# Decay attention and mixture of experts on one core: the listed order of all steps and the buffers laid out anew

## The chip, the core and the metric

The kernel runs on one core of a Trainium2 chip. The metric is the device time of one execution in microseconds; shorter is better. The core has five engines with queues of their own: TensorE (PE in the rows; PEld is its loading of weights, which overlaps the matmuls), VectorE (DVE), ScalarE (ACT), GpSimd (POOL) and SyncE (SP), which here only issues transfers. An engine takes its queue in order; an instruction that waits for another engine holds up all that stand behind it on its own.

## The reference

Attention with a decay over 8 batches of 8 heads (576 positions, 64 wide), and on its output a mixture of 4 experts, of which each position takes 2, each an attention of its own. Cut to what matters:

```python
# attention: q, k, v (8, 8, 576, 64), f (8, 8, 576)
scores = scale * np.matmul(q, k.transpose(0, 1, 3, 2))
cum = np.cumsum(np.log(np.clip(f, 0.0001, 1.0)), axis=-1)
scores = np.where(causal, -1000000000.0, scores + cum[..., :, None] - cum[..., None, :])
attn = softmax(scores)
x = np.matmul(attn, v)                      # laid out as (8, 576, 512)
# experts: top 2 of 4 by x @ w_gate, w = softmax over the two logits
for e in range(4):
    q, k, v = x @ wq[e], x @ wk[e], x @ wv[e]
    a = softmax(np.where(causal, -1000000000.0, scale * (q @ k.T)))
    ye = a @ v @ wo[e]
    for kk in range(2):
        out += (topk[:, :, kk] == e)[..., None] * w[:, :, kk:kk + 1] * ye
```

## The kernel before

The work is cut into 48 units. 32 are a batch and a pair of heads (a0_0 to a7_3: batch, pair), 16 a batch and a pair of experts (m0_0 to m7_1). The experts of a batch come one batch behind its heads. Each unit goes through the same steps, and each step is a Python generator, a task:

- `prep_attn` (L396) loads xin (L401), copies halves of it with ScalarE (L404, L407; L410 only in the first two units) and takes the rounding remainders with two VectorE operations of 64 partitions each (L416). Their two halves, near and far, start on partition 0 and on partition 64, in one order or the other. SP copies halves within SBUF (L394) and adds rows for the decay (L386 for the first unit, L390 for the others). `prep_moe` (L526) does the like for experts, with matmuls pp_m (L542).
- `max_pass` (L563) finds each row's maximum: matmuls m0, m1, m2, m3 (all L571, shown as m_a or m_m), each followed by a VectorE reduction (L577, with a short read of its accumulator under the same line, and L592, L624, L631), then a transpose mp on TensorE (L636) and a copy ms on ScalarE (L639).
- `scores` (L660) multiplies again (L670, L671), exponentiates on ScalarE (L687 to L726), masks on GpSimd (L657, L690, L728) and adds up the blocks there (L734 to L740).
- `attend` (L746) multiplies by the values: oa and ob (both L759). `row_sums` (L789) and `apply_rows` (L840) divide a group of two units by its sums: matmuls sm (L798), VectorE L812 to L830, ScalarE L832, L869, VectorE L850, L877.
- `moe_front` (L429) makes the experts' values (pv, L445) and gates (L464 to L523). `project_out` (L881) multiplies by wo (po, L893), copies to outb with ScalarE (L900) and stores (L903, L906).

Beside the units, `load_weights` loads and splits the weights (st_v, st_k and so on: SP L359, ScalarE L363, GpSimd L365), and `keep_warm` (L215) issues 150 matmuls on zeros (warm, L218) that nobody reads.

What sets the order is no scheduler but a table. ORDER is a string of two-digit numbers to the base 64; each names a task and advances it by one step, to its next `yield` (4w is `keep_warm`, 00 the `prep_attn` of a0_0, 4A `load_weights`). A loop behind it makes every instruction depend on the one before it on its engine, so that each engine's queue stands as listed. SLOTS says, for each kind of tile, which of its buffers the next allocation takes; an allocation waits until the last reader of that buffer is done. Both tables come from a replay of the program outside of the kernel; the kernel holds only its result.

```python
digits = "".join(ORDER.split())
for x, y in zip(digits[::2], digits[1::2]):
    i = DIGITS.index(x) * len(DIGITS) + DIGITS.index(y)
    if i not in started:
        started[i] = iter(tasks[i]())
    next(started[i], None)
```

Of the kernel before, what the change touches and what calls it, by code (L numbers as in the profile page):

```python
# [1003 lines left out]
```

## Time and profile before

| | us |
|---|---|
| runs of the kernel before | 703.61, 706.12, 706.38 |
| their median | 706.12 |
| the profiled execution | 704.02 |
| its span, first to last instruction | 702.3 |
| TensorE busy in it | 675.6 |
| VectorE busy in it | 575.9 |
| GpSimd busy in it | 454.4 |
| ScalarE busy in it | 448.3 |

The profile is of one execution. Times in rows count from the span's start. Tiles are shown by kind: ka_a stands for the ka tile of any attention unit, so the unit is told by the position. A name in brackets behind a row, [1.90 <-PE m_a L571], says how long the engine was idle ahead of it and what ended that. Matmuls overlap, and their ends are modelled: a busy TensorE may still run below its peak.

### The profile page before, as it was taken

To read this page: it belongs to the slowest core of one execution; us is meant where nothing else is said; L and a number is where in the kernel's file an instruction comes from. 1 tells how busy PE (TensorE), PEld (TensorE's weight loads), DVE (VectorE), ACT (ScalarE), POOL (GpSimd) and SP (SyncE) were. 2 spreads that over 40 slices of the span, in tenths; PEclk is the share of its full clock that TensorE was granted. 3 is DMA by queue.
4 is the path that set the end of the run, shared out by engine and by line. 5 is a ranking of instruction groups with operands and counts; after the bars stand their busy time and mean duration, and the time that the engine had idled before them with its cause. 6 is when DMAs were issued, how large, how long until landed. Compare 5 with 4: busy or idle time off the path is not lost.

```text
span 702.3 us, 15565 instructions
## 1 busy us (share of the span) xinstructions
PE 675.6 (96%) x5470; PEld 562.1 (80%) x5470; DVE 575.9 (82%) x1664; ACT 448.3 (64%) x961; POOL 454.4 (65%) x760
## 2 busy tenths in 40 slices
PE   8988999889999999999999999999999999999997
PEld 7665888668888889779787898788887797879874
DVE  6979978988889789978989878978898998685752
ACT  5676747665677756766585856586567764656454
POOL 8589586668675764685657746746676766643470
PEclk9999999999999999999999999999999999999999
DMA  5756333441335332453333424353334242222203
GB/s 162 198 147 179 105 84 109 104 107 39 95 105 159 104 88 81 124 158 88 112 88 101 121 56 139 87 136 86 109 103 122 68 124 52 75 64 50 50 17 120
DMA packets 31231, 72.25 MB, mean 103 GB/s; under 512 B 4137, under 2 KB 4617, under 8 KB 31153
## 3 DMA queue, kind: packets, MB, share of 16 engines
q1 hardware_dynamic: 31153, 71.25, 36.8%
q8 instruction: 43, 0.70, 0.4%
q14 instruction: 35, 0.29, 0.1%
HBM read 32.91 MB, written 10.35 MB: 62 GB/s over the span
## 4 chain that ended last, share of the span: by engine, by line
PE 68%; DVE 18%; ACT 4%; issue 4%; DMA 3%; POOL 2%; SPq 0%; DVEq 0%; ACTq 0%; POOLq 0%
PE pp_m L542 12%; PE pv L445 7%; PE m_a L571 6%; PE po L893 6%; DVE ka_a L416 6%; PE s_a L670 5%; PE s_a L671 5%; PE ob_a L759 5%; PE ob_m L759 4%; PE m_m L571 4%; DVE junk_a L577 3%; PE s_m L670 3%; PE s_m L671 3%; PE oa_a L759 2%; PE sm_a L798 2%
## 5 line engine op out<-in xcount | busy, mean ns | idle before, releaser
L577 DVE CUSTOM_DVE_ANT_0 junk_a<-m_a,mask 128x448 bf16<-128x448 f32 (+2 forms) x192 | 91.9, 486 | 22.0 <-PE m_a L571 15.3
L670 PE MATMUL s_a<-ka_a 128*128 128x320 f32 (+4 forms) x384 | 106.3, 301 | 1.1 <-DMA ka_a<-kq 0.6
L657 POOL TENSOR_SCALAR_AFFINE_SELECT P_a<-P_a 128x128 f32<-128x128 f32 x128 | 49.4, 391 | 84.9 <-ACT P_a L705 42.3
L671 PE MATMUL s_a<-kq 128*128 128x320 f32 (+4 forms) x384 | 103.2, 294 | 0.3 <-DMA kq<-ms_a 0.3
L571 PE MATMUL m_a<-kq 128*128 128x320 f32 (+4 forms) x384 | 92.0, 312 | 9.0 <-DVE mxs_a L577 6.6
L571 PEld LDWEIGHTS m_a<-kq 128*128 128x128 f32 (+1 forms) x384 | 61.8, 181 | 22.7 <-DVE mxs_a L577 12.3
L555 DVE TENSOR_TENSOR ka_m<-pp_m,kq 64x288 fp32r<-64x288 f32 x128 | 58.2, 455 | 25.3 <-ACT kq L550 20.5
L734 POOL TENSOR_TENSOR R_a<-P_a 128x448 f32<-128x448 f32 x64 | 76.4, 1195 | 0.0
L670 PEld LDWEIGHTS s_a<-ka_a 128*128 128x128 f32 (+1 forms) x384 | 69.3, 180 | 7.6 <-issue 2.8
L550 ACT ACTIVATE kq<-pp_m 64x288 fp32r<-64x288 f32 x128 | 51.8, 405 | 32.0 <-PE pp_m L542 30.1
L671 PEld LDWEIGHTS s_a<-kq 128*128 128x128 f32 (+1 forms) x384 | 68.7, 181 | 1.5 <-DMA kq<-ms_a 0.7
L759 PE MATMUL ob_a<-P_a,va 128*64 128x320 f32 (+1 forms) x512 | 67.6, 406 | 0.2 <-ACT ot_a L785 0.2
L736 POOL TENSOR_TENSOR R_a<-R_a,P_a 128x320 f32<-128x320 f32 x64 | 64.5, 1008 | 3.7
L687 ACT ACTIVATE P_a<-s_a 128x512 f32<-128x512 f32 x64 | 37.3, 597 | 31.1 <-PE s_a L671 30.7
L759 PEld LDWEIGHTS ob_a<-P_a,va 128*64 128x64 f32 x512 | 35.8, 137 | 24.4 <-ACT ot_a L785 0.4
L670 PE MATMUL s_m<-ka_m 128*128 128x192 f32 (+2 forms) x192 | 53.4, 302 | 0.0
L671 PE MATMUL s_m<-kq 128*128 128x192 f32 (+2 forms) x192 | 52.1, 298 | 1.0 <-DMA kq<-ms_m 1.0
L577 DVE CUSTOM_DVE_ANT_0 junk_m<-m_m,mask 128x192 bf16<-128x192 f32 (+2 forms) x96 | 45.8, 484 | 7.7 <-PE m_m L571 6.4
L738 POOL TENSOR_TENSOR R_a<-R_a,P_a 128x192 f32<-128x192 f32 x64 | 48.7, 763 | 4.0
L416 DVE TENSOR_TENSOR ka_a<-xin_a,kq 64x1152 fp32r<-64x1152 f32 x32 | 49.9, 1561 | 1.2 <-ACT kq L404 0.3
L657 POOL TENSOR_SCALAR_AFFINE_SELECT P_m<-P_m 128x128 f32<-128x128 f32 x64 | 20.3, 320 | 45.9 <-ACT P_m L705 27.4
L416 DVE TENSOR_TENSOR ka_a<-xin_a,ka_a 64x1152 fp32r<-64x1152 f32 x32 | 49.0, 1532 | 0.9
(191 smaller groups left out, 2122.8 us busy)
## 6 DMA issues: line engine op xcount, KB each, us to landing
xin_a<-in_qk_dram SPq DMA_DIRECT2D x32, 576.0 KB
va<-in_v_dram SPq DMA_DIRECT2D x32, 320.0 KB
ka_a<-kq SPq DMA_DIRECT2D x32, 288.0 KB
ka_m<-kq SPq DMA_DIRECT2D x32, 288.0 KB
kq<-ka_a SPq DMA_DIRECT2D x30, 288.0 KB
out_dram<-outb SPq DMA_DIRECT2D x32, 256.0 KB
kq<-ex SPq DMA_DIRECT2D x47, 27.0 KB
kq<-ms_a SPq DMA_DIRECT2D x64, 2.5 KB
```

The source lines that it names most:

```text
L416: nc.vector.tensor_tensor(lo, x[at], hi.bitcast(F32), ALU.subtract)
L542: nc.tensor.matmul(pp[:, :HS], w[:, c, es], x[c][:, gs], start=(n == 0), stop=(n == 3 * KC - 1))
L550: nc.scalar.activation(hv[h], src[h], AF.Copy)
L555: nc.vector.tensor_tensor(lo[:, h, gs], src[h], hv[h].bitcast(F32), ALU.subtract)
L571: nc.tensor.matmul(dst, qB[0:K, h, i0 : i0 + dst.shape[0]], kB[0:K, h, j0:j1], start=True, stop=True)
L577: nc.vector.tensor_tensor_reduce(jk[:, :n], src, mask[:, MW - n :], 1.0, init, ALU.add, ALU.max, acc)
L657: return nc.gpsimd.affine_select(pv, pv, [[1, 128]], ALU.is_ge, 0.0, base=0, channel_multiplier=-1)
L670: nc.tensor.matmul(dst, kaf[:, c : c + m], qA[:, h, i0:i1], start=True, stop=False)
L671: nc.tensor.matmul(dst, kqf[0:K, c + h * S : c + h * S + m], qB[0:K, h, i0:i1], start=False, stop=True)
L734: g.tensor_tensor(r[:, h, 128:S], q[:, 320:768], q[:, 768:1216], ALU.add)
L736: g.tensor_tensor(r[:, h, 256:S], r[:, h, 256:S], q[:, 1216:1536], ALU.add)
L759: mm = nc.tensor.matmul(dst[64 * h : 64 * h + 64, c0 : c0 + rhs.shape[-1]], vs[h][0:kp, blk], rhs, start=first, stop=last,)
```

## The change

Only the two tables are changed. All 97 lines of ORDER's digits are replaced, and in SLOTS the rows of P, xin, xh, mxs, psm, pss, ol, psx, xl and outb. The functions, the tiles and the number of instructions on each engine stay as they are, apart from waits that stand alone (on PE 191 before and 204 now, DVE 245 and 227, ACT 148 and 158, SP 241 and 237, POOL 31 and 22). The replay that gave the new tables lets an operation that works on other partitions than the one before it on its engine start only when that one has ended.

```diff
 DIGITS = "0123456789abcdefghijklmnopqrstuvwxyzABCDEFGHIJKLMNOPQRSTUVWXYZ+-"
 ORDER = """
...
-00024A4A074w4w4w4w4w4w4w4w4w4w004w020500004z02024w4w020202024w4w4w4w4w4w020202024w4w4z020202020202024z4A024A4A
...
+4w4w4w0100004w004z4z4z4w0200020202024w4w4z0202024w024w4w4w4w4w4w024w0202024y4y4y4y4y4y4y024w4w4w4w024w0202020c4w
...
 SLOTS = """
...
-outb 010101010101010101010101010
+outb 010101010111101010111111111
```

What this moves is seen on the engines' queues. The first place is SP's queue at the start of the program: fl is the input of the decay, xin_a0_0 to xin_a0_2 the first units' inputs, st_ the weights, chl the finished decay rows, ex the rows for later units, va0 the first unit's values. Before:

```order
L286 DMA fl_118<-in_f_dram 64x576
L401 DMA xin_a0_0_241<-in_qk_dram 128x1152
L359 DMA st_v0_249<-in_wv_dram 128x512
L401 DMA xin_a0_1_251<-in_qk_dram 128x1152
L386 DMA kq0_108<-chl_120 2x1x576 x2
L314 DMA ex_117<-chl_120 64x2x576
L316 DMA ex_117<-neg_124 64x2x576
L318 DMA ex_117<-one_121 64x1152
L359 DMA st_v1_328<-in_wv_dram 128x512
L359 DMA st_v2_335<-in_w_gate_dram 128x16
L359 DMA st_k0_361<-in_wk_dram 128x512
L390 DMA kq1_109<-ex_117 3x2x1152
```

Now:

```order
L286 DMA fl_118<-in_f_dram 64x576
L401 DMA xin_a0_0_200<-in_qk_dram 128x1152
L401 DMA xin_a0_1_215<-in_qk_dram 128x1152
L359 DMA st_v0_228<-in_wv_dram 128x512
L359 DMA st_v1_232<-in_wv_dram 128x512
L359 DMA st_v2_236<-in_w_gate_dram 128x16
L359 DMA st_k0_242<-in_wk_dram 128x512
L359 DMA st_k1_246<-in_wk_dram 128x512
L424 DMA va0_101<-in_v_dram 128x640
L386 DMA kq0_108<-chl_120 2x1x576 x2
L314 DMA ex_117<-chl_120 64x2x576
L316 DMA ex_117<-neg_124 64x2x576
```

The weights st_v1 to st_k1 and va0 moved ahead of the two transfers kq0<-chl of line 386. On TensorE, 94 warm-ups stand ahead of the first m0_a0_0 before and 87 now; between the last matmul of that max pass and its transpose mp_a0_0 stand 24 before and 4 now, and the next 16 behind it.

The second place is VectorE's queue where the max pass of a0_3 ends and that of a1_0 begins. Before:

```order
L577 ISA junk_a0_3_727,mxs_a0_3_511<-m3_a0_3_725,mask_95 128x320
L577 ISA mxs_a0_3_511 128x1
L416 TENSOR_TENSOR ka_a1_0_674<-xin_a1_0_544,kq0_108 64x1152
L577 ISA junk_a1_0_770,mxs_a1_0_756<-m0_a1_0_767,mask_95 128x192
L577 ISA mxs_a1_0_756 128x1
L592 TENSOR_REDUCE mxt_a1_0_778<-m0_a1_0_767 128x1
L577 ISA junk_a1_0_783,mxs_a1_0_756<-m0_a1_0_780,mask_95 128x192
L577 ISA mxs_a1_0_756 128x1
L592 TENSOR_REDUCE mxt_a1_0_778<-m0_a1_0_780 128x1
L577 ISA junk_a1_0_812,mxs_a1_0_756<-m1_a1_0_792,mask_95,mxt_a1_0_778 128x256
L577 ISA mxs_a1_0_756 128x1
L416 TENSOR_TENSOR ka_a1_0_674<-xin_a1_0_544,ka_a1_0_674 64x1152
```

Now:

```order
L577 ISA junk_a0_3_735,mxs_a0_3_605<-m3_a0_3_733,mask_95 128x320
L577 ISA mxs_a0_3_605 128x1
L416 TENSOR_TENSOR ka_a1_0_683<-xin_a1_0_531,kq0_108 64x1152
L416 TENSOR_TENSOR ka_a1_0_683<-xin_a1_0_531,ka_a1_0_683 64x1152
L577 ISA junk_a1_0_778,mxs_a1_0_646<-m0_a1_0_774,mask_95 128x192
L577 ISA mxs_a1_0_646 128x1
L592 TENSOR_REDUCE mxt_a1_0_780<-m0_a1_0_774 128x1
L577 ISA junk_a1_0_787,mxs_a1_0_646<-m0_a1_0_782,mask_95 128x192
L577 ISA mxs_a1_0_646 128x1
L592 TENSOR_REDUCE mxt_a1_0_780<-m0_a1_0_782 128x1
L577 ISA junk_a1_0_812,mxs_a1_0_646<-m1_a1_0_805,mask_95,mxt_a1_0_780 128x256
```

The second L416 of a1_0 moved up from behind the first m1 reduction of a1_0 to right behind the first L416.

The third place is VectorE's queue where the max pass of a2_0 begins; rc, zt and rr are tiles of the row sums of a1_2 and a1_3. Before:

```order
L577 ISA junk_a2_0_1987,mxs_a2_0_1560<-m0_a2_0_1976,mask_95 128x192
L577 ISA mxs_a2_0_1560 128x1
L815 TENSOR_SCALAR rc_a1_2_1989<-zt_a1_2_1965 128x18
L416 TENSOR_TENSOR ka_a2_1_1960<-xin_a2_1_1684,kq3_111 64x1152
L817 RECIPROCAL rc_a1_2_1989<-rc_a1_2_1989 128x18
L592 TENSOR_REDUCE mxt_a2_0_2013<-m0_a2_0_1976 128x1
L824 CAST zt_a1_2_1965<-rc_a1_2_1989 128x18
L416 TENSOR_TENSOR ka_a2_1_1960<-xin_a2_1_1684,ka_a2_1_1960 64x1152
L826 TENSOR_TENSOR zt_a1_2_1965<-rc_a1_2_1989,zt_a1_2_1965 128x18
L577 ISA junk_a2_0_2029,mxs_a2_0_1560<-m0_a2_0_2015,mask_95 128x192
L577 ISA mxs_a2_0_1560 128x1
L592 TENSOR_REDUCE mxt_a2_0_2013<-m0_a2_0_2015 128x1
```

Now:

```order
L577 ISA junk_a2_0_1991,mxs_a2_0_1737<-m0_a2_0_1977,mask_95 128x192
L577 ISA mxs_a2_0_1737 128x1
L592 TENSOR_REDUCE mxt_a2_0_2011<-m0_a2_0_1977 128x1
L830 STREAM_TRANSPOSE rr_a1_2_2014<-zt_a1_2_1898 128x576
L577 ISA junk_a2_0_2022,mxs_a2_0_1737<-m0_a2_0_2016,mask_95 128x192
L577 ISA mxs_a2_0_1737 128x1
L592 TENSOR_REDUCE mxt_a2_0_2011<-m0_a2_0_2016 128x1
L577 ISA junk_a2_0_2063,mxs_a2_0_1737<-m1_a2_0_2025,mask_95,mxt_a2_0_2011 128x256
L577 ISA mxs_a2_0_1737 128x1
L416 TENSOR_TENSOR ka_a2_1_2019<-xin_a2_1_1686,kq3_111 64x1152
L416 TENSOR_TENSOR ka_a2_1_2019<-xin_a2_1_1686,ka_a2_1_2019 64x1152
```

The two L416 of a2_1 moved from among the m0 reductions of a2_0 to behind its first m1 reduction, and the row sums L815 to L826 to ahead of the first m0 reduction. On TensorE, the attend of m0_0 (oa, ob) and the first four pairs of score matmuls of m0_1 now stand between the first and the second m1 matmul of a2_0.

## Rows read from the trace of the kernel before

**Rows 1.** The page: busy time and share of each engine; TensorE clock by slice.
```profile
PE 675.6 (96%) x5470; PEld 562.1 (80%) x5470; DVE 575.9 (82%) x1664; ACT 448.3 (64%) x961; POOL 454.4 (65%) x760
...
PEclk9999999999999999999999999999999999999999
```

**Rows 2.** Two long stretches: length, each engine's busy us (instructions), clock, DMA share, GB/s.
```profile
14.00:170.00 156.00, 143.26 (x1135) 114.68 (x1134) 136.90 (x380) 101.21 (x203) 112.03 (x178) 0.99 0.47 126
170.00:699.00 529.00, 519.62 (x4243) 436.82 (x4241) 430.45 (x1275) 338.16 (x751) 329.79 (x555) 1.00 0.34 95
```

**Rows 3.** Chain that ended last, long pieces: start, us, engine, tile, line, count.
```profile
47.23 0.80 PE oa_a L759 x8
48.03 2.06 PE ob_a L759 x20
...
101.99 1.11 PE sm_a L798 x16
...
174.15 1.59 PE pp_m L542 x12
```

**Rows 4.** Timeline of TensorE at the start: start, us, engine, line, operation, tiles.
```profile
13.71 0.50 PE L571 MATMUL m_a<-kq 128*128 128x192 f32 x2
...
18.69 2.79 PE L218 MATMUL warm<-wz 128*128 128x256 bf16 x24
21.32 0.27 PE L636 MATMUL mp_a<-ident,mxs_a 128*10 128x128 f32 x1
```

**Rows 5.** Timeline of ScalarE at the start: last operation before the first max pass.
```profile
10.50 1.16 ACT L410 ACTIVATE kq<-xin_a 64x1152 fp32r<-64x1152 f32 x1
```

**Rows 6.** Three stretches of the start, columns as in rows 2.
```profile
3.00:7.60 4.60, 4.60 (x31) 3.56 (x30) 3.45 (x5) 0.93 (x3) 4.42 (x6) 1.00 0.77 301
7.60:9.10 1.50, 1.50 (x17) 1.34 (x15) 0.75 (x1) 1.50 (x2) 1.31 (x9) 1.00 0.00 0
9.10:12.80 3.70, 3.70 (x36) 3.32 (x34) 2.71 (x2) 3.63 (x4) 3.49 (x6) 1.00 0.26 59
```

**Rows 7.** Timeline of VectorE, 22 to 30 us: same partitions, then other partitions.
```profile
23.03 0.49 DVE L592 TENSOR_REDUCE mxt_a<-m_a 128x1 f32<-128x320 f32 x1
23.44 0.35 DVE L577 CUSTOM_DVE_ANT_0 junk_a<-m_a,mask 128x192 bf16<-128x192 f32 x1
...
28.28 1.51 DVE L416 TENSOR_TENSOR ka_a<-xin_a,kq 64x1152 fp32r<-64x1152 f32 x1
29.82 1.45 DVE L416 TENSOR_TENSOR ka_a<-xin_a,ka_a 64x1152 fp32r<-64x1152 f32 x1
```

**Rows 8.** Timeline of VectorE around a1_0's two L416 [idle before it <- releaser].
```profile
47.44 1.35 DVE L416 TENSOR_TENSOR ka_a<-xin_a,kq 64x1152 fp32r<-64x1152 f32 x1
50.70 0.36 DVE L577 CUSTOM_DVE_ANT_0 junk_a<-m_a,mask 128x192 bf16<-128x192 f32 x1 [1.90 <-PE m_a L571]
...
52.57 1.44 DVE L416 TENSOR_TENSOR ka_a<-xin_a,ka_a 64x1152 fp32r<-64x1152 f32 x1
...
67.82 2.10 DVE L877 TENSOR_TENSOR xl_a<-ot_a,xh_a 128x576 fp32r<-128x576 f32 x1 [1.45 <-ACT xh_a L869]
```

**Rows 9.** Timeline of ScalarE: the L407 of a1_0.
```profile
44.10 1.17 ACT L407 ACTIVATE ka_a<-xin_a 64x1152 fp32r<-64x1152 f32 x1
```

**Rows 10.** Timeline of VectorE around a2_1's two L416.
```profile
135.09 2.04 DVE L416 TENSOR_TENSOR ka_a<-xin_a,kq 64x1152 fp32r<-64x1152 f32 x1
...
138.76 1.35 DVE L416 TENSOR_TENSOR ka_a<-xin_a,ka_a 64x1152 fp32r<-64x1152 f32 x1
```

**Rows 11.** Timeline of GpSimd beside them.
```profile
135.05 0.86 POOL L736 TENSOR_TENSOR R_m<-R_m,P_m 128x320 f32<-128x320 f32 x1
...
138.76 2.07 POOL L736 TENSOR_TENSOR R_m<-R_m,P_m 128x320 f32<-128x320 f32 x1
```

**Rows 12.** Timeline of TensorE there: the longest wait for VectorE.
```profile
142.01 0.61 PE L571 MATMUL m_a<-kq 128*128 128x256 f32 x2 [1.85 <-DVE mxs_a L577]
```

**Rows 13.** VectorE's L416 alone, 14 to 170 us: length, busy us (instructions).
```profile
14.00:170.00 156.00, 32.93 (x21) 0.99 0.47 126
```

More of the change, by code (lines that the diff above doesn't have):

```diff
@@ new lines @@
+4w4w4w4w4y4y4w4w07020202024w4w024A4y054w4w0205054w4w4w4w4w4w4w4w4w4w4w4w4w4w4w4w050502054A0c000c0202070703070307
+07070707030307070707070303030307070705070c0c07034z0e4w0h07074w034z074z034w4w4w4w4w4w4w4w4w4w03070707074w0c0e4w0c
+4w030303030303074w030e0d0e060e03034w0303034w4w0o0h0h030e0h4w030h4w0808080e0e080e0e0h0e0e0e03040h03030e08080e040e
+0108030c0j0e0e0e0e0h0o080808080e08080j080e0e0e0e0j08040e0q080803080j0j0j0e080j080808080t080j0j0j0j0j0o080j08080f
+0f080j0f4z0f0f0j0j0j0j0j0f080o0f0f0f0j0j0j0t0o0o0f0j090j0f0j090o0o0f0f084x0f0v0q080q0q0q0j0j0q0q0f0f0f0f0f0f0q0k
@@ new lines @@
+0q0f0f0q0f0k0k0q0q0q0k0A0t0t090f0f0q0k0k0k0t0t0t0t0k0a0a0q0a0a0k0k0q0a0f0q0q0a0q0k0f0k0a0k0g0q0p0A0g0f0k0f0q0g0v
+0a0q0q0v0a0k0k0k0k0k0k0k0v0v0v0k4A0v0v0i0k0k0k0v0b0q0F0q0q0q0b0b0b0v0f0A0v0v0v0l0b0k0k0k0k0b0v0v0A0A4A0v0b0f0r0b
+0v0l0k0C0v0v0k0r0r0v0b0r0r0r0r0v0v0b0C0r0r0r0v0r0r0v0v0r0b0b0r0m0v0v0C0C0r0r0l0r0r0r0m0m0m0r0b0u0C0m0m0m0m0r0r0C
+0r0r0C0C0F0w0w0A0r0r0r0w0C0w0w0r0m0N0s0n0F0n0w0n0w0r0w0C0n0w0C0n0C0C0C0M4w0n0w0w0w0H0w0w0w0C0n0n0n0M0M0C0C0n0n0C
+0C0n0n0w0w0w0w0w0w0w0w0w0w0s0N0N4A0C0F0F0N0H0C0N0s0C0M0x0N0N0C0C0H0N0N0H0r0r0A0A0C0M0H4A0C0C0M0M0R0M4w0H0M0N0N0H
@@ new lines @@
+0M0F0M0M0H0H0N0N0N0F0N0N0D0D0H4A0D0D0D0D0N0O0N0H0N0N0N0w0w0N0w0w0N0N0N0D0N0N0N0D0H0H0H0N0N0H0F0w0D0D0w0H0N0G0N0N
+0H0M0H0M0N0N0D0M0H4A0N0D0D0D0H0M0M0H0M0x0H0D0H0O0y0y0O0H0y0y0H0D0D0O0R0b0O0D0D0y0O0y0H0D0D0D0D0O0O0O0D0y0y0D0R0R
+0R0R0H0D0D0M0Y0D0N0O0R0y0O0M0M0R0R0M0M0I0I0I0I0I0I0D0M0z0z0O0B0D0Y0z0z0O0O0I0O4A0I0R0I0z0M0M0O0O0O0M0I0M0M0M0M11
+0O0O0M0M0M0M0M0M0M0M0a0z0z0O0R0R0N0I0I0I0I0I0I0R0x0O0O0z0R0R0+0R0I0I0I0I0I0I0I0I0I0I0I0I0I0I0I0R0M0M4A0Y0E0O0R0E
+110z0z0E0O0O0O0z0Y0Y0Y0Y0R0R0R0R0R0R0R0R0R0R0R0R0R0R0R0R0R0R0R0z0D180R0J0z0S0M0M0J0S0S0P0S0M0S0P0P0P0J0P0S0S0S0K
@@ new lines @@
+0S0K0M0M0K0K0S0S0K0P0S0P0P0S0P0P0S0S0P0P0K0S0S0S0S0S0P0P0P0P0S0P0P0S0K4z0P0P0P0P0P0+0S0P0P0P0P0P0S0S0S0S0+0M180+
+0K0+110E110+0+0+0Q0Q110K0y0T0T0T0T0T0T0Q0+0H110+110+0+0+0P0+0T000+0T0+0T0M0+1d0T0T0T0T0T0T0+0+0+0M0P0+0T130T130T
+120+0T0+0T0T4w0+0Y130T0T130L0T0T0T0L0T0L0L130+0+0+0u0L0L1313130T0T130P0U0-13180T0T0-0L131313130-0-0-0-0L0L130-13
+13131318180L0L0-0-0-0-13130-0Z0-130V0L0-0V13130V0L130-1a0-1a1a1d0V0-0-0-1a0-0-0-0-1a111a1a0V1f1k0V0V0V130V1k1k1k
+191k1k140-0-1k141k0V131a1k1k141a1k0U0U1k1k1a1a1a1a1a140-0-0-1k0W14141414141a1l0W0W140W141k1a1k1k0W1a1l1k1d1d1a1a
@@ new lines @@
+1414141414144A4A1l1a1l0W1l1l1d141a1k1k1k1l1k1k1818141k1a141414141418101l1a0W1a1a1l1f1d1a1k1a1f1f1k1k1k1d0-1f1f1f
+1f1d1k130V4A0-1p1l1l1k1f1b1l1l1l1b1f1f1b1b1l1l1l1l1w1m0W0W1f1f101f4A14141l1l1b1b1b1l101l1f14141f1b1k1l1l1l1b1b1b
+1b1l1l1l1b1b1b1l14141l1l141f1k1k1k1l1l1k1f1e1f1f1f1l1l1f1l1l0W1b1b1b1b1k1b1b1b1b050-0W1f15151k1k161k1k16161f1m1m
+1f1p1m161616161p0W0W161p1p1B1b1m1m1m1p1p1b1f1p1m1g1f1m1p1g1g1p1p161g1p1g1p1l1p1p1m1m1m1m1m1p1b1g1g1p1q1b1p1b0n1b
+1b1b1g1w1p1g1g1g1m1p1p0W1m1m171p171p1m1p1m1m1m1p151p1m1m1g1p1p1p0W0W0W1x1p1p1p1g1p1g0G1g1g1g1g1g1m1g1g1m1m1m1g1q
@@ L128 @@
 R 201210210210210210210210210210210210210210210210210
 pso 0101010101010101010101010101010101010101010101010101010101010101010101010101010101010101010101010
[L130 removed]
+xin 01010101010101011001010101101001
 ka 012012012012012012012012012012012012012012012012
[L132 to L134 removed]
+xh 01234501234540123534012534012534012534012
```

184 lines of the change are left out of this document (78 added, 106 removed).

## Prediction

> **What bounds the kernel now.** I read the page first: TensorE is busy 96% of the span, VectorE 82%, and the granted clock is full in every slice [rows 1]. An average over stages says little, so I cut the span where its character changes. From 14 to 170 us VectorE is idle for 156.00 − 136.90 = 19.1 us and TensorE for 12.7 us; from 170 to 699 us TensorE is idle for only 529.00 − 519.62 = 9.4 us, VectorE for 98.6 us [rows 2]. So both engines set the pace in the first stretch, and TensorE alone in the second.
>
> A busy TensorE is not TensorE at its peak, so I priced its list. Twelve pp_m matmuls of 288 columns take 1.59 us: 0.46 ns a column. A unit's attend takes 0.80 + 2.06 = 2.86 us and one row-sum group 1.11 us [rows 3]. From 170 to 699 us run 770,108 columns of the first sort (354 us), 37 units' attends (106), 19 row-sum groups (21) and 4 us of small ones: 485 us, an estimate. The stretch lasts 529, so TensorE loses up to 44 us in waits, of which rows 2 show 9.4 as idle. The list could gain something between those two.
>
> **The change, part by part.** Every engine has the same instructions in both kernels, apart from pure waits on semaphores; nothing is removed. What moves is who stands ahead of whom.
>
> *Start.* The first matmul of the first max pass runs at 13.71 us [rows 4], though ScalarE had its last input ready at 10.50 + 1.16 = 11.66 [rows 5]: 94 warm-up matmuls are listed ahead of it. Now 87 are. 24 of them take 2.79 us [rows 4], 0.116 each, so 7 give −0.8 us. From there the transpose mp_a0_0 also stands behind 4 warm-ups instead of 24, but its followers wait for VectorE, so I count nothing more; at best, down to the ready input, it is −2. On SP's queue five weight loads and the values (st_v1, the gate weights, st_k0, st_k1, va0: 1,096 KB) are now listed ahead of the two L386 transfers that the first max pass needs. Before, the DMA engines do nothing from 7.60 to 9.10 us and little until 12.80 [rows 6]. At the 301 GB/s of the stretch before [rows 6] these loads take 3.7 us and end near 11.3, ahead of the warm-ups' end near 12.9: no cost, the idle engines are the cover. At the 126 GB/s of the next stretch [rows 2] they would take 8.9 us, end at 16.5 and cost 2.8 us. I take −0.8 (−2 to +2), since the first rate is that of large loads alone, as here; the loads they replace later leave the queue freer between 14 and 35 us.
>
> *The VectorE-bound stretch.* Both L416 of a1_0 now stand together. Before, the first ends at 47.44 + 1.35 = 48.79, then VectorE waits 1.90 us for TensorE's m_a, which stands behind the attend of a0_1 (2.86 us, rows 3); the second L416 (1.44 us) comes only after four reductions and the first m1, at 52.57 [rows 8]. Its input, ScalarE's L407, has been there since 45.27 [rows 9]. Put into the 1.90 us gap, it costs nothing: −1.4 us. What is late next is the 1.45 us wait for ScalarE's xh at 67.82 [rows 8]; if ScalarE comes no earlier, that wait eats the gain, so the bound is 0. The other place is a2_0, where two L416 and the row sums of a1_2 stand among the first four reductions: VectorE is at it from 135.09 to 138.76 + 1.35 = 140.11, and TensorE waits 1.85 us, the longest wait I found [rows 10, 12]. Now the row sums come earlier, and the L416s come after the first m1 reduction, with the 2.86 us attend of m0_0 and the first scores of m0_1 ahead of the m1 matmul that they hold up. There a wait on TensorE goes, but VectorE has the same work, so I count only 0.5 us for this and all places like it. Together −1.9; the ends are 0 (the work is merely pushed) and −6 (a third of the 19.1 us).
>
> *Partitions.* The change's name says that an operation on other partitions waits for its forerunner's end. The rows show it: L577 on the same partitions starts at 23.44, before L592 ends at 23.52; L416 on partitions 64 on starts at 29.82, 0.03 us after its forerunner's end at 29.79 [rows 7]. A switch costs 0.08 + 0.03 = 0.11 us. But the lists hold nearly as many: neighbours in the order of which one touches partition 64 fall from 386 to 376 on VectorE. Ten by 0.11 are 1.1 us, of which the part that lies in VectorE's stretch, 156 of 702 us [rows 2], keeps 0.2. I take −0.2 (0 to −1.1).
>
> *TensorE's waits after 170 us.* For each matmul that awaits a result I compared the work listed on the producing engine since its forerunner with the work listed on TensorE meanwhile. Places short by over 0.3 us fall from 82 to 64 in this stretch, a fifth. A fifth of the 9.4 us shown idle is −1.9, a fifth of 44 is −8.8. I take −3.5, nearer to the waits that rows show; 0 if the waits only change place.
>
> *Buffers.* The slots of the output tile outb repeat one number nine times in a row near the end where they alternated. ScalarE then waits for a store before the next copy. ScalarE is idle for 529.00 − 338.16 = 190.8 us after 170 [rows 2], which covers it; uncovered, nine waits of a microsecond or two would undo the term above.
>
> *Sum.* −0.8 − 1.9 − 0.2 − 3.5 = −6.4 us. The profiled execution took 704.02 us, so 697.6; the median of the runs, 706.12, lies 2.1 above it: **699.7 us**.
>
> **The rivals.** *The waits only move: about 706.* The start's −0.8 stays and the rest nets to nothing: 705.3. For it: four fifths of the short places are still there, and the gain at 50.70 can be eaten at 67.82. Against it: the gap at 50.70 is plainly filled.
>
> *GpSimd and VectorE collide more: slower.* Beside GpSimd's adds an L416 takes 2.04 us instead of 1.35, or the add takes 2.07 us instead of 0.86 [rows 10, 11]: one seems to hold the other up whole. [...] The new order sets every L416 against other adds. From 14 to 170 us 21 of them take 32.93/21 = 1.57 us [rows 13]. At 2.04 each they cost 9.9 us more, at half of that 5.0. With the first and third terms kept and the second and fourth lost, half of it gives 704.0 − 1.0 + 5.0 = 708.0, or **710** as a median; all of it 715. It turns slower by 0.5% (3.5 us) once the mean passes 1.57 + 4.5/21 = 1.78 us. Against it: two L416 in a row meet fewer adds than two apart.
>
> *The list gains in full:* −2 − 6 − 1.1 − 8.8 = −17.9, a median of **688**.
>
> *The change hardly does what it says:* the partition rule as such moves almost nothing (386 to 376), which is why its term is small. The gain, if there is one, is that of a list laid out anew.
>
> **How the numbers follow.** The forecast case (696 to 703) has 0.47, the moved waits 0.25, the collision 0.16, the full gain 0.12. A run of this kernel can tell about 0.5% from no change, 702.6 and 709.7 being the bounds. Faster takes the full gain and nearly all of the forecast case: 0.55. The moved waits, the rest of the forecast case and a third of the collision make the same: 0.31. Slower is the rest of the collision and a mishap in the start: 0.14. The range runs from 690, where the full gain's better half is left out, to 711, past half of the collision; about 0.06 lie below and 0.1 above.
>
> **What would show it.** Right: the first m_a near 12.9 us; both L416 of a1_0 back to back ahead of the m_a reductions and no 1.9 us gap behind them; VectorE idle in 14 to 170 us below 18; TensorE's end earlier by more than at 170 us, which splits the sum into its terms. Wrong: DMA share well above 0.3 between 9 and 13 us with the first m_a later than 13.7; a mean L416 above 1.78 us in the first stretch; ScalarE's L900 waiting for stores with TensorE's po behind it; or landmarks at 170 us as before and the stretch after it still 529 us long.

## The result, and the profile after

The changed kernel takes **698.59 us** (median of 4 runs, 697.36 to 699.17), the kernel before beside it 705.44 us (4 runs, 703.61 to 706.38). The ratio is 0.9904, with an interval of 0.9877 to 0.9930: faster by 1.0%. The profiled execution took 698.17 us, its span is 696.5 us. In all later comparisons the kernel before had medians of 703.61 to 704.25; against those the gain would be 5.0 to 5.6 us instead of 6.9.

The page of the changed kernel, as [rows 1]: TensorE's busy time falls from 675.6 to 672.2 us, and its granted clock is no longer full everywhere.

```profile
PE 672.2 (97%) x5470; PEld 562.0 (81%) x5470; DVE 579.8 (83%) x1664; ACT 447.2 (64%) x961; POOL 458.2 (66%) x760
...
PEclk9998999999999999999999999999999999999999
```

The two long stretches, as [rows 2]: length, busy us and instructions of PE, PEld, DVE, ACT and POOL, granted clock, DMA share, GB/s. The shorter program puts some other work into the same limits, so this view alone doesn't split the gain.

```profile
14.00:170.00 156.00, 145.86 (x1138) 117.52 (x1137) 133.95 (x381) 102.21 (x206) 112.58 (x188) 0.97 0.42 115
170.00:699.00 529.00, 513.57 (x4246) 434.10 (x4245) 437.32 (x1274) 335.42 (x743) 335.17 (x553) 1.00 0.35 97
```

To split it I price each matmul of the trace by its columns, warm-ups apart, and add the prices up in order of time. At the same sum two kernels have done the same amount of TensorE's work, whatever its order. The first two columns are that sum and the time at which the kernel before reaches it; the others say how much later (+) or earlier (−) another kernel does. The other kernels are the experiments below.

```
work us  before   after  after_then_  before_then_  values_
                         before       after         late
   5      30.15    -1.8    -2.2         +0.3          -1.8
  15      44.49    +2.1    +4.2         +0.3          -2.2
  45      82.72    +2.6    +2.8         +3.1          -4.3
  90     131.80    +2.4    +2.6         +3.1          -4.5
 120     169.82    -0.3    -0.2         +1.7          -7.3
 250     308.27    -1.9    +0.7         -0.2          -9.1
 400     470.46    -3.9    +0.3         -2.4         -11.1
 608     696.56    -6.1    +0.1         -4.7         -15.2
```

So the first stretch, up to 170 us, gives only 0.3 us, after a loss of some 4 us between 30 and 45 us, and the stretch behind it gives 5.8 us. Three questions follow: what eats the gain of the first stretch, whether the gain behind 170 us comes from the list there, and what a change of partitions costs.

**The loss.** SyncE's queue in the changed kernel (start, us, line, operation): the values va2 and va1 (L424) are listed ahead of xin_a1_0 (L401). Before, only one va stood there.

```profile
31.03 0.89 SPq L424 DMA_DIRECT2D va<-in_v_dram  x2
32.02 0.37 SPq L401 DMA_DIRECT2D xin_a<-in_qk_dram  x1
```

The timelines of ScalarE, TensorE and VectorE there (in brackets the idle time ahead and what ended it): ScalarE waits 4.64 us for that input, where it waited 0.98 us before (first row, of the kernel before); TensorE then waits 3.15 us, VectorE 3.90 us.

```profile
36.22 1.17 ACT L404 ACTIVATE kq<-xin_a 64x1152 fp32r<-64x1152 f32 x1 [0.98 <-DMA xin_a<-in_qk_dram]
```
```profile
39.49 1.16 ACT L404 ACTIVATE kq<-xin_a 64x1152 fp32r<-64x1152 f32 x1 [4.64 <-DMA xin_a<-in_qk_dram]
```
```profile
41.19 0.69 PE L670 MATMUL s_a<-ka_a 128*128 128x448 f32 x1 [3.15 <-ACT P_a L699]
```
```profile
42.88 0.36 DVE L577 CUSTOM_DVE_ANT_0 junk_a<-m_a,mask 128x192 bf16<-128x192 f32 x1 [3.90 <-PE m_a L571]
```

Windows of 5 us, columns as above: after the gap the granted clock is 0.66, and later, behind a second thin stretch, 0.52 and 0.80.

```profile
35.00:40.00 5.00, 3.04 (x27) 2.20 (x23) 3.81 (x11) 0.51 (x1) 4.86 (x7) 1.00 0.87 236
40.00:45.00 5.00, 3.81 (x16) 3.30 (x16) 1.54 (x6) 3.32 (x9) 1.33 (x5) 0.66 0.04 16
...
60.00:65.00 5.00, 3.83 (x31) 2.69 (x27) 4.87 (x19) 2.02 (x5) 3.85 (x6) 1.00 0.94 305
65.00:70.00 5.00, 4.85 (x22) 2.95 (x22) 3.96 (x12) 3.98 (x9) 4.26 (x8) 0.52 0.13 42
70.00:75.00 5.00, 5.00 (x37) 3.63 (x34) 1.79 (x9) 1.15 (x3) 3.84 (x8) 0.80 0.23 52
```

Sixteen matmuls ob_a of one form take 2.11 us at 59.56, where the clock is 1.00, and 3.71 us at 68.78, most of it in the low stretch:

```profile
59.56 2.11 PE L759 MATMUL ob_a<-P_a,va 128*64 128x320 f32 x16
...
68.78 3.71 PE L759 MATMUL ob_a<-P_a,va 128*64 128x320 f32 x16
```

If TensorE's rate falls with the granted clock, five us at 0.66, 0.52 and 0.80 are by estimate at most 1.7 + 2.4 + 1.0 = 5.1 us of lost TensorE time. The kernel before loses at most 1.3 + 0.4 = 1.7 us in the same way:

```profile
140.00:145.00 5.00, 3.15 (x13) 2.48 (x12) 4.32 (x16) 2.11 (x4) 2.43 (x5) 0.75 0.98 256
145.00:150.00 5.00, 4.38 (x32) 3.47 (x34) 3.80 (x15) 2.52 (x8) 2.97 (x8) 0.91 0.08 18
```

This holds beyond the one profile: the mean granted clock was 0.989 to 0.993 in all four runs of the changed kernel, and 0.993 to 1.000 in the runs of the kernel before beside the experiments.

### The profile page after: what moved, and what is told of

Read it like the earlier page. It is cut to its first block, busy times and chain, and to the rows that moved or that the text cites. A ratio compares the mean times of both kernels' runs of the same rounds, so it can differ in the third digit from the quotient of the medians.

```text
span 696.5 us, 15557 instructions
## 1 busy us (share of the span) xinstructions
PE 672.2 (97%) x5470; PEld 562.0 (81%) x5470; DVE 579.8 (83%) x1664; ACT 447.2 (64%) x961; POOL 458.2 (66%) x760
## 4 chain that ended last, share of the span: by engine, by line
PE 75%; DVE 15%; DMA 3%; issue 3%; ACT 2%; POOL 2%; DVEq 0%; SPq 0%; ACTq 0%
PE pp_m L542 12%; PE ob_a L759 8%; PE pv L445 7%; PE m_a L571 6%; PE po L893 6%; PE s_a L670 6%; PE s_a L671 5%; DVE ka_a L416 4%; PE m_m L571 3%; PE ob_m L759 3%; PE oa_a L759 3%; PE s_m L670 3%; PE s_m L671 3%; DVE junk_a L577 2%; PE sm_a L798 2%
## 5 line engine op out<-in xcount | busy, mean ns | idle before, releaser
L657 POOL TENSOR_SCALAR_AFFINE_SELECT P_a<-P_a 128x128 f32<-128x128 f32 x128 | 47.3, 375 | 100.2 <-ACT P_a L705 55.4
L577 DVE CUSTOM_DVE_ANT_0 junk_a<-m_a,mask 128x192 bf16<-128x192 f32 (+2 forms) x192 | 91.7, 485 | 25.0 <-PE m_a L571 23.0
L734 POOL TENSOR_TENSOR R_a<-P_a 128x448 f32<-128x448 f32 x64 | 74.8, 1169 | 0.0
L759 PE MATMUL ob_a<-P_a,va 128*64 128x320 f32 (+1 forms) x512 | 69.2, 413 | 0.0
L416 DVE TENSOR_TENSOR ka_a<-xin_a,ka_a 64x1152 fp32r<-64x1152 f32 x32 | 50.8, 1586 | 1.0
L416 DVE TENSOR_TENSOR ka_a<-xin_a,kq 64x1152 fp32r<-64x1152 f32 x32 | 48.8, 1524 | 1.0
L690 POOL TENSOR_SCALAR_AFFINE_SELECT P_a<-P_a 128x256 f32<-128x256 f32 x64 | 35.6, 565 | 21.1 <-ACT P_a L687 20.8
L445 PE MATMUL pv<-vh,xh_a 128*128 128x260 f32 x160 | 46.5, 290 | 1.9 <-DVE lg L464 1.6
```

Of the source, the lines that this page charges most:

```text
L416: nc.vector.tensor_tensor(lo, x[at], hi.bitcast(F32), ALU.subtract)
L445: nc.tensor.matmul(pv[:, :NV], l[c][:, t0 : t0 + 128], r[:, c], start=(n == 0), stop=(n == 3 * KC - 1))
L577: nc.vector.tensor_tensor_reduce(jk[:, :n], src, mask[:, MW - n :], 1.0, init, ALU.add, ALU.max, acc)
L734: g.tensor_tensor(r[:, h, 128:S], q[:, 320:768], q[:, 768:1216], ALU.add)
L759: mm = nc.tensor.matmul(dst[64 * h : 64 * h + 64, c0 : c0 + rhs.shape[-1]], vs[h][0:kp, blk], rhs, start=first, stop=last,)
```

## Experiments

All kernels start from the changed one (the joined lists from both), and none leaves work out. In all of them the slots of R, the row sums' partial adds, differ from the changed kernel's, in some those of a few other kinds of tile too. hold_same, whose order is untouched, ran at 698.97 us, so the slots of R alone gain nothing. Medians in us; the kernel before is that of the same comparison.

| kernel | median (lowest to highest, runs) | ratio to before | interval |
|---|---|---|---|
| xin_first | 693.59 (689.64 to 696.22, 6) | 0.9842 | 0.9814 to 0.9870 |
| xin_first_again | 697.65 (694.17 to 698.68, 6) | 0.9903 | 0.9880 to 0.9926 |
| fill_gap | 697.24 (694.60 to 700.84, 6) | 0.9908 | 0.9884 to 0.9931 |
| xin_first_fill | 695.53 (692.59 to 695.96, 5) | 0.9887 | 0.9873 to 0.9901 |
| before_then_after | 698.15 (695.30 to 700.53, 6) | 0.9909 | 0.9887 to 0.9930 |
| after_then_before | 704.16 (702.58 to 705.57, 11) | 0.9997 | 0.9986 to 1.0007 |
| split_a1_0 | 699.67 (694.03 to 700.68, 5) | 0.9932 | 0.9905 to 0.9959 |
| hold_same | 698.97 (697.94 to 702.27, 6) | 0.9943 | 0.9923 to 0.9964 |
| hold_other | 707.90 (704.78 to 711.02, 7) | 1.0065 | 1.0041 to 1.0089 |
| three_moves | 696.88 (692.65 to 698.96, 6) | 0.9894 | 0.9867 to 0.9920 |
| values_late | 690.29 (689.17 to 691.41, 6) | 0.9797 | 0.9770 to 0.9824 |
| values_late_fill | 691.40 (687.95 to 693.51, 6) | 0.9804 | 0.9774 to 0.9835 |

### xin_first and xin_first_again: the late input

One row of SyncE's queue moves up:

```diff
+L401 DMA xin_a1_0<-in_qk_dram 128x1152
 L424 DMA va2<-in_v_dram 128x640
 L424 DMA va1<-in_v_dram 128x640
-L401 DMA xin_a1_0<-in_qk_dram 128x1152
```

> The changed kernel with one transfer moved: on SyncE's queue the load xin_a1_0 stands ahead of the value loads va2 and va1 instead of behind them. In the changed kernel's trace it is issued at 32.02 us and lands at about 39.5, ScalarE waits 4.64 us for it and TensorE 3.15 us for ScalarE, and the clock is at 0.66 from 40 to 45 us. Theory 1 (the two value loads ahead of it make xin late, and this wait is the loss of the first stretch): the load is issued near 31.0 and lands near 36, ScalarE's wait falls below 1.5 us and TensorE's 3.15 us wait goes; the kernel gains 2 to 3.5 us over the changed one, 695 to 696.5. Rival (the DMA engines are full there whatever the order, or VectorE takes the time back before 170 us): the wait goes or moves to the values, and the kernel stays at 698.6 within 1 us.

The input lands at 33.3 us instead of 39.5, and ScalarE's wait of 4.64 us is gone. The median is 5.0 us below the changed kernel's. But the load that was delayed before has a successor: TensorE now waits 1.84 us for the first max matmul of a0_3, whose operand kq is completed by transfers that stand behind va2 and va1. Timeline of TensorE in xin_first (its line numbers are two higher):

```profile
38.81 0.50 PE L573 MATMUL m_a<-kq 128*128 128x192 f32 x2 [1.84 <-DMA kq<-ka_a]
```

> The kernel of xin_first once more, to stand beside three_moves on the same chip, and for another profile. Its six runs lay at 690 to 692 us (clock 1.000) and at 695 to 696 (0.993 to 0.995). Expected again: a median of 690 to 696; if this profile is of the upper group, its clock shows where TensorE ran at the lower level. Theory 1b has that near 60 us.

The same list gave 697.65 in another comparison, on another chip: only 0.9 us below the changed kernel. Its profile shows what goes with the difference: the same wait lasts 2.50 us, and the clock falls behind it, as it did behind the 3.15 us of the changed kernel and did not behind the 1.84 us above.

```profile
40.68 0.82 PE L573 MATMUL m_a<-kq 128*128 128x192 f32 x2 [2.50 <-DMA kq<-ex]
```
```profile
40.00:45.00 5.00, 3.73 (x15) 3.08 (x16) 2.03 (x8) 2.30 (x7) 1.52 (x7) 0.56 0.12 28
45.00:50.00 5.00, 5.00 (x20) 4.83 (x21) 2.56 (x10) 2.32 (x4) 4.84 (x7) 0.50 0.83 230
```

The three executions with a mean clock of 1.000 took 689.6 to 692.1 us, the one at 0.998 took 694.2, those at 0.989 to 0.995 took 695.1 to 698.7. The length of one wait doesn't decide it: in the kernel before, the window at 0.75 shown above holds a wait of 1.85 us [rows 12]. So moving one load removes the wait that it caused, but shifts it to the next transfer behind the values, and the medians, 5.0 and 0.9 us apart from the changed kernel's, don't agree on a gain.

### fill_gap and xin_first_fill: TensorE kept busy

In fill_gap, 28 more warm-up matmuls are listed where TensorE waits at 38 us; in xin_first_fill, 34 in four such places of xin_first.

```diff
+    def fill():
+        wps = ptile(ps_x, "x", "fill")
+        for _ in range(28):
+            nc.tensor.matmul(wps[:, :256], wz[:, 0:128], wz[:, :256], start=True, stop=True)
+            yield
```

> The changed kernel with 28 more warm-up matmuls (about 3.2 us of TensorE work that nobody reads), listed where TensorE waits 3.15 us near 38 us. The wait itself stays. Theory 1 (the wait costs twice, by itself and by the low clock behind it): the clock stays at 1.00 from 40 to 45 us, and 1 to 1.5 us of the loss come back by 50 us; 697 to 698. Rival (VectorE sets the pace there, so a slower TensorE costs nothing): clock at 1.00, but the same time within 0.5 us, 698.6; or, if the wait ends earlier than the filling, slower by up to 0.5 us.

With the wait filled the clock holds, there and in the later stretch too. Windows of fill_gap:

```profile
40.00:45.00 5.00, 3.99 (x26) 3.45 (x27) 2.97 (x12) 4.30 (x11) 3.00 (x8) 1.00 0.14 43
...
65.00:70.00 5.00, 5.00 (x45) 3.93 (x46) 3.40 (x11) 3.08 (x6) 4.84 (x7) 1.00 0.30 69
260.00:265.00 5.00, 5.00 (x40) 3.18 (x40) 0.00 (x0) 0.00 (x0) 0.00 (x0) 0.66 0.01 2
```

From work 5 to work 35 it gains 3.4 us on the changed kernel. Then it gives 3.4 us back near 260 us, where TensorE waits 3.18 us for the values of another unit (1.5 us in the changed kernel) and the clock falls behind that wait. From 260 to 265 us VectorE, ScalarE and GpSimd stand idle until TensorE's results come.

```profile
259.74 0.62 PE L768 MATMUL oa_a<-P_a,va 128*64 128x256 f32 x3 [3.18 <-DMA va<-in_v_dram]
```

The median is 697.24: the clock can be held, but this alone shows no gain in the runs.

> The kernel of xin_first (the load xin_a1_0 ahead of va2 and va1) with 34 more warm-up matmuls that nobody reads, listed in four places between 36 and 60 us where TensorE waits 0.4 to 2.0 us in its trace. The runs of xin_first fell into two groups: 690 to 692 us with the clock at 1.000 over the span, 695 to 696 with 0.993 to 0.995. Theory 1b (the second group is a stretch of low clock behind the thinly filled TensorE near 60 us): the fillings hold the clock, all runs lie in the first group, median 690 to 692. Rival (the low clock comes elsewhere, or the first group is a matter of the chip's start): two groups as before, median 693 to 694; if the fillings outlast the waits, 0.5 to 1 us more.

It failed as an improvement: the mean clocks are 0.996 to 1.000, but near 42 us the fillings outlast the wait and cost 1.3 us, and the median is 695.53 instead of 690 to 692.

### before_then_after and after_then_before: which half gains

The two lists are joined at the transpose mp_a2_1, near 150 us: one kernel has the order of before up to there and the changed order behind it, the other the reverse. The edit is to the digits of ORDER, here of the first kernel against the changed one:

```diff
 ORDER = """
...
-4w4w4w0100004w004z4z4z4w0200020202024w4w4z0202024w024w4w4w4w4w4w024w0202024y4y4y4y4y4y4y024w4w4w4w024w0202020c4w
...
+00024A4A074w4w4w4w4w4w4w4w4w4w004w020500004z02024w4w020202024w4w4w4w4w4w020202024w4w4z020202020202024z4A024A4A
...
```

> The list of the kernel before up to its transpose mp_a2_1 (157 us), and behind it the changed list without the steps done; buffers laid out for it. Theory 2 (the gain of 6 us is made behind 160 us, by the list there, and the two parts add): the gain up to the cut is 0, behind it 5 to 6 us; 698.6 to 700. Rival (the gain behind the cut hangs on how far GpSimd, ScalarE and the loads have come at the cut, so it needs the changed first part too): less than half of it, 702 to 705.

> The other way round: the changed list up to its transpose mp_a2_1 (155 us) and the list of before behind it. Theory 2: at the cut 1 us ahead of before, and no gain behind it: 704 to 705.5. Rival (the first part prepares the gain): 700 to 702.

The parts add: −5.9 us (698.15 against 704.0) and +0.2 us (704.16) beside the whole change's −5.4 against the same 704.0. From 170 us on, before_then_after gains 6.4 us and the whole change 5.8, while after_then_before loses 0.3. The gain comes with the changed list behind the cut, and the clock has no part in it: the granted clock behind 170 us is 1.00 before and after. The mean clock was 0.990 to 0.993 in all 11 runs of after_then_before and 0.992 to 0.997 in those of before_then_after, so it is lowest with the changed order's first stretch. But that order isn't the only one to lose it: before_then_after, with the order of before up to the cut, also shows 0.73 from 60 to 65 us and 0.79 from 70 to 75 in its profile.

### split_a1_0: the pairing undone

VectorE's queue at a1_0 as it stood before:

```diff
 L416 TENSOR_TENSOR ka_a1_0<-xin_a1_0,kq0 64x1152
-L416 TENSOR_TENSOR ka_a1_0<-xin_a1_0,ka_a1_0 64x1152
 L577 ISA junk_a1_0,mxs_a1_0<-m0_a1_0,mask 128x192
...
 L577 ISA mxs_a1_0 128x1
+L416 TENSOR_TENSOR ka_a1_0<-xin_a1_0,ka_a1_0 64x1152
```

> The changed kernel with its second place undone: the second L416 of a1_0 back behind the first m1 reduction of a1_0. The prediction's step gave the pairing 1.4 us. If it holds, the trace at equal TensorE work is 1 to 1.5 us later between 55 and 80 us than the changed kernel's, 700 at the end or swallowed by 170 us. Rival (the gap that the pairing filled is no longer there, since a1_0's m0 is late for another reason, the late xin): no difference, 698.6 within 0.5 us, and a gap of over 1 us on VectorE ahead of m0.

The gap comes back as predicted. VectorE of the changed kernel, as [rows 8], where 0.20 us of the wait is left behind the pair:

```profile
49.71 1.39 DVE L416 TENSOR_TENSOR ka_a<-xin_a,kq 64x1152 fp32r<-64x1152 f32 x1
51.13 1.45 DVE L416 TENSOR_TENSOR ka_a<-xin_a,ka_a 64x1152 fp32r<-64x1152 f32 x1
52.77 0.36 DVE L577 CUSTOM_DVE_ANT_0 junk_a<-m_a,mask 128x192 bf16<-128x192 f32 x1 [0.20 <-PE m_a L571]
```

and of split_a1_0:

```profile
50.03 1.35 DVE L416 TENSOR_TENSOR ka_a<-xin_a,kq 64x1152 fp32r<-64x1152 f32 x1
53.33 0.36 DVE L577 CUSTOM_DVE_ANT_0 junk_a<-m_a,mask 128x192 bf16<-128x192 f32 x1 [1.95 <-PE m_a L571]
...
55.21 1.35 DVE L416 TENSOR_TENSOR ka_a<-xin_a,ka_a 64x1152 fp32r<-64x1152 f32 x1
```

At equal work split_a1_0 is 0.7 us earlier than the changed kernel ahead of this place and 1.4 us later from work 35 to the end: 2.1 us. Not all of that is the pairing's: from 45 to 50 us its granted clock was 0.63 where the changed kernel's was 1.00, up to 1.9 us of TensorE time. The medians differ by 1.1 us with intervals that overlap. So the gap is shown to come and go with the pairing; the 1.4 us that I gave it are neither confirmed nor denied.

### hold_same and hold_other: the price of other partitions

96 memsets of one column stand behind the reductions of line 592, on partitions 0 to 63 in hold_same and 64 to 127 in hold_other. The work is the same; only hold_other adds 2 × 96 = 192 changes of partition.

```diff
+            s = next(spares)
+            nc.vector.memset(spare[0:64, s : s + 1], 0.0)
```

> The changed kernel with 96 one-column memsets on VectorE, two in each max pass, each behind an L592, on a spare tile's partitions 0 to 63: the partitions where its neighbours start too. It is the base for hold_other. Each should cost what such an operation takes, some 0.06 us, and only where VectorE sets the pace: 698.6 to 700.

> The same 96 memsets on partitions 64 to 127 of the spare tile, so that each, and the operation behind it, starts on other partitions than its forerunner. Theory 3, from the prediction's step on partitions (0.11 us for a switch, and only VectorE's stretch up to 170 us pays): 192 switches make VectorE 21 us busier or idler over the span, but the kernel only 2 to 5 us slower than hold_same, 701 to 704; in the trace the memset starts 0.02 to 0.03 us after its forerunner's end instead of 0.08 ahead of it. Rival a (VectorE is on the path throughout): 10 us or more. Rival b (a switch costs nothing that reaches the end): as hold_same within 0.5 us.

Timeline of VectorE in hold_same: the memset starts 0.05 us before its forerunner ends (21.48 + 0.48 = 21.96).

```profile
21.48 0.48 DVE L594 TENSOR_REDUCE mxt_a<-m_a 128x1 f32<-128x320 f32 x1
21.91 0.06 DVE L596 MEMSET spare<- 64x1 f32 x1
```

In hold_other it starts 0.06 us after it (22.60 + 0.48 = 23.08), and the next operation starts 0.01 us behind the memset's end (23.14 + 0.06 = 23.20).

```profile
22.60 0.48 DVE L594 TENSOR_REDUCE mxt_a<-m_a 128x1 f32<-128x320 f32 x1
23.14 0.06 DVE L596 MEMSET spare<- 64x1 f32 x1
23.21 0.36 DVE L579 CUSTOM_DVE_ANT_0 junk_a<-m_a,mask 128x192 bf16<-128x192 f32 x1
```

So 0.11 us of overlap are lost at an instruction. At the kernel's end the medians differ by 707.90 − 698.97 = 8.9 us, 0.047 us for each of 192 changes. This understates the price, since hold_other had the fuller clock: 0.990 to 1.000 in its runs against 0.984 to 0.993. At a mean clock of 0.990 it took 710.90 us against 699.02 and 698.21, at 0.993 709.71 against 697.94: some 12 us, 0.06 us for each change. My 2 to 5 us were too low, and the 10 us of rival a are reached.

I had expected the price where VectorE sets the pace. At equal work hold_other is 0.5 us behind at work 45 and 1.0 at 120, then 3.6 at 250, 6.1 at 350 and 8.9 at the end. Up to 170 us hold_same lost more to the clock (0.96 from 14 to 170 us against 0.98, up to some 3 us), so the price there may be up to 4 us. Still most of it is paid behind 170 us, where both have the full clock and VectorE is idle for 80 to 90 us:

```profile
170.00:699.00 529.00, 514.37 (x4252) 434.77 (x4250) 439.36 (x1345) 336.29 (x745) 335.84 (x554) 1.00 0.35 97
```
```profile
170.00:699.00 529.00, 517.11 (x4247) 433.51 (x4246) 449.31 (x1346) 336.09 (x745) 334.07 (x554) 1.00 0.35 94
```

(hold_same first). VectorE's average leaves room, but reductions that the next matmul awaits have none: behind 170 us the waits of TensorE's weight loads for VectorE's maxima rise from 2.9 to 5.9 us (m_a) and from 1.5 to 3.9 us (m_m).

### three_moves: more gain from the waits left over

On top of xin_first, three steps behind 150 us that the trace shows waiting are listed some places later, so that TensorE does other work first. One of them:

```diff
-L571 MATMUL m_a3<-kq3 128x256
 L670 MATMUL s_a2<-ka_a2 128x192
 L671 MATMUL s_a2<-kq2 128x192
...
+L571 MATMUL m_a3<-kq3 128x256
```

> The kernel of xin_first with three local moves, each at a TensorE wait of its trace: ScalarE's rt of m0_0 (L832) behind the copy vm of batch 1 that TensorE waits for through its buffer (wait of 1.63 us at 155 us); the attend of a3_1 behind a row sum, a transpose and one score pair, since it waits 1.69 us for GpSimd's mask at 256 us; the first m1 matmul of a5_3 behind two score pairs (1.11 us at 411 us). Theory 2b (behind 150 us the time is the sum of such waits on TensorE, each worth itself): 3 to 4 us less than xin_first. Rival (the work put ahead was needed as cover a little later, so the waits come back within some 10 us): within 1 us of xin_first.

Nothing: the median of 696.88 us is 0.8 below that of xin_first_again beside it, within the rival's 1 us. At equal work it stays 0.1 us from the changed kernel from work 40 to 160 and ends 0.6 us later. In its trace the first wait still stands (1.63 us at 162 us, for VectorE's lg), the second is gone but one of 1.57 us for ka_m follows at 264 us, and only the third is gone without another near it. These three single moves don't find what the whole list found.

### values_late and values_late_fill: the values behind what is awaited

Both values move behind the transfers that are needed first. SyncE's queue:

```diff
-L424 DMA va2<-in_v_dram 128x640
-L424 DMA va1<-in_v_dram 128x640
 L401 DMA xin_a1_0<-in_qk_dram 128x1152
 L394 DMA kq3<-ka_a0_3 64x2x576
 L390 DMA kq3<-ex 3x2x1152
 L394 DMA ka_a0_2<-kq2 64x2x576
 L394 DMA ka_a0_3<-kq3 64x2x576
+L424 DMA va1<-in_v_dram 128x640
 L394 DMA kq2<-ms_a0_2 1x5x128 x2
 L401 DMA xin_a1_1<-in_qk_dram 128x1152
+L424 DMA va2<-in_v_dram 128x640
```

> The changed kernel with two transfers moved: on SyncE's queue the value load va1 stands behind the copies for a0_3 (kq3, ka_a0_3) and va2 behind the load xin_a1_1, so that xin_a1_0 and the two kq3 transfers come 640 KB earlier. In xin_first the load xin_a1_0 landed at 33 to 35 us, ScalarE's wait of 4.64 us was gone, but TensorE then waited 1.84 and 2.50 us for kq3, which landed at 38.4 to 40.4. Theory 1c (between 30 and 42 us the DMA engines are full, and the two value loads, wanted only behind 45 us, are what stands in the way): kq3 lands near 36 to 37, TensorE's wait near 38 us falls below 0.5 us, the clock stays at 1.00 from 40 to 55 us, and the runs lie together at 689 to 693. Rival (what is late then is VectorE or the copies themselves): a wait of 1.5 us or more stays there, 694 to 698.

690.29 us, with a mean clock of 0.996 to 1.000 in every run: some 8 us faster than the changed kernel (698.59 in another comparison) and 14 us (2.0%) faster than the one before beside it. SyncE issues the input at 31.05, the copy of kq at 33.62; both land in time.

```profile
31.05 0.38 SPq L401 DMA_DIRECT2D xin_a<-in_qk_dram  x1
33.62 0.67 SPq L394 DMA_DIRECT2D kq<-ka_a  x1
...
36.48 0.78 SPq L424 DMA_DIRECT2D va<-in_v_dram  x1
```

From 36 to 41 us the only wait of over 0.2 us that TensorE shows is this, and the clock stays full:

```profile
39.00 0.28 PE L636 MATMUL mp_a<-ident,mxs_a 128*10 128x128 f32 x1 [0.26 <-DVE mxs_a L577]
```
```profile
35.00:40.00 5.00, 4.68 (x36) 3.49 (x31) 4.49 (x14) 3.46 (x7) 4.92 (x8) 1.00 0.96 230
40.00:45.00 5.00, 4.42 (x33) 3.79 (x34) 3.85 (x16) 4.14 (x9) 4.77 (x11) 1.00 0.57 194
```

From 35 to 40 us the DMA engines are as full as in the changed kernel (0.96 against 0.87), and all bytes are the same: only the order differs. At equal work it has gained 4.3 us on the changed kernel by work 15 and 6.9 by work 35, which is about the size of that one's losses there, gaps and low clock together. fill_gap left the wait and held the clock, and gained 3.4 us over the same stretch: by that estimate about half of the loss is the clock's. Another 1.9 us come between work 400 and the end; their cause is not shown.

> values_late with 12 more warm-up matmuls that nobody reads, 9 and 3 of them at two waits of TensorE near 58 and 60 us. Theory 1b, what is left of it (the thinly filled TensorE near 60 us is followed by a stretch at the lower level in some runs): the clock over the span is 0.998 or more in all runs, and the upper runs of values_late, if there are any, are missing; otherwise as values_late. Rival: the runs spread as without the fillings, and lie up to 1 us higher.

Twelve warm-ups more, in the thin stretch near 59 us, add nothing: 691.40 us, with mean clocks of 0.997 to 1.000. The clock was held already.

## Why the prediction held, point by point

The forecast of 699.7 us met 698.59, yet two of its terms were wrong by about the same amount, in opposite directions: the first stretch gave 2.6 us less than its terms, the stretch behind it 2.3 us more. That the sum came so near is luck.

**The start**, predicted −0.8: −0.2 in the pair of profiles, right within its range. The first m_a ran at 13.54 us, not near 12.9. Seven warm-ups fewer did save their 0.8 us, but another cost came in. At the start of the program a warm-up takes 0.21 us and later 0.11 (last section). The step came at 5.9 us in the profile before and at 7.1 in this one, and 1.2 us at half the rate cost 0.6. My 0.116 us was read from late warm-ups [rows 4], and [rows 1, 6] give the full clock for the first microseconds too, where the warm-ups ran at half that rate. The step's time isn't the list's: in xin_first, with the same list up to there, it came at 3.9 us, and m_a ran at 11.97. The five loads moved ahead (four of weights and the values, not five of weights as I wrote) cost nothing, though the DMA share from 9.10 to 12.80 us was 0.51: m_a waits for no transfer.

```profile
13.54 0.76 PE L571 MATMUL m_a<-kq 128*128 128x192 f32 x4
```
```profile
9.10:12.80 3.70, 3.70 (x36) 3.31 (x35) 2.66 (x2) 3.65 (x7) 1.45 (x1) 1.00 0.51 158
```

**The VectorE-bound stretch**, predicted −1.9: the gap closed as I said, its worth isn't shown. The 1.90 us of [rows 8] are 0.20, and split_a1_0 brings them back. The place at a2_0 [rows 10] changed too: both L416 stand behind the m1 reduction, and the wait of [rows 12] is gone.

```profile
139.73 1.40 DVE L416 TENSOR_TENSOR ka_a<-xin_a,kq 64x1152 fp32r<-64x1152 f32 x1
141.16 1.64 DVE L416 TENSOR_TENSOR ka_a<-xin_a,ka_a 64x1152 fp32r<-64x1152 f32 x1
```

Between work 90 and work 100, where this place lies, the changed kernel gains 2.8 us on the one before, up to 1.7 us of it the dip in the clock that the latter has there. Even so the whole first stretch, start and partitions included, came to −0.3 instead of −2.9, and the sign "VectorE idle in 14 to 170 us below 18" failed: it was idle for 156.00 − 133.95 = 22.1 us, where it was 19.1. The step that failed is the sentence on the start's loads: "the loads they replace later leave the queue freer between 14 and 35 us". I checked SyncE's queue where the diff's first place shows it and assumed the rest. There, at 31 us, two values were moved ahead of an input that ScalarE was about to need. The rows for it were in the order of the queues, not in the trace of before. values_late shows that this ate the gain: a wait of 3.15 us and the clock behind it. My terms held no price for the clock.

**Partitions**, predicted −0.2 of at most −1.1: ten switches at the measured 0.05 to 0.06 us are −0.5 to −0.6 by estimate, too small to be seen. The price of an instruction, 0.11 us, was right. Wrong was the step that kept only the share inside VectorE's stretch: hold_other pays most behind it.

**TensorE's waits after 170 us**, predicted −3.5 in 0 to −8.8: −5.8. That the changed list gains here is shown by before_then_after; that it gains by fewer waits for results is not. A fifth of the idle time would have been −1.9, a fifth of all that TensorE loses −8.8, and I leaned to the first, since rows show it. But the idle time that rows show did not shrink. From work 120 to work 608 TensorE is idle for 526.74 − 517.61 = 9.1 us before and 520.94 − 511.89 = 9.1 us now; all that was saved lies in time that the view calls busy. Before, then now:

```profile
169.82:696.56 526.74, 517.61 (x4236) 435.55 (x4235) 430.63 (x1275) 337.56 (x749) 329.97 (x555) 1.00 0.34 94
```
```profile
169.52:690.46 520.94, 511.89 (x4242) 433.17 (x4242) 437.79 (x1275) 334.52 (x742) 335.65 (x554) 1.00 0.36 96
```

Nor did the waits for VectorE's maxima fall there. From 170 to 699 us (total, times, longest) they are, before and now:

```profile
PE m_a L571 <- DVE mxs_a L577: 1.1, 2, 0.9
```
```profile
PE m_a L571 <- DVE mxs_a L577: 2.1, 3, 1.2
```

Ahead of the weight loads they are 2.7 and 2.9 us. Over the whole program they do fall, from 6.6 to 3.7 us ahead of the matmuls and from 12.3 to 6.6 ahead of the weight loads, but that is the first stretch's. So matmuls follow each other a little sooner in time shown as busy, and what lets them stays open. three_moves found no single place to add.

**Buffers**, uncosted: right, as far as the trace of the changed kernel shows. What ended ScalarE's waits at L900 in the changed kernel (us, times) was TensorE, and never a store:

```profile
  PE po L893: 12.8, 14
  DMA xin_a<-in_qk_dram: 0.2, 1
```

**The rivals.** The collision is refuted: L416 alone, as [rows 13], takes 28.70/20 = 1.44 us in the first stretch, below the 1.57 of before and far from 1.78. Over 14 to 699 us its busy time is 96.8 us where it was 96.3.

```profile
14.00:170.00 156.00, 28.70 (x20) 0.97 0.42 115
```

"The waits only move" was true of three_moves and of the idle time shown behind 170 us; the time itself fell. "The list gains in full", at 688, didn't come, but it was nearer than it looks: values_late, which takes one bad place out of the list, runs at 690.29. "The change hardly does what it says" was true of the partitions as far as their estimate goes, and false of the list.
